# Attention followed by a soft mixture of experts: turned score maxima kept in a score tile's spare columns, a fifth exponential buffer, and PSUM places chosen by two clocks

## The chip, the core and the metric

The kernel runs on one core of one Trainium2 chip. The metric is the device time of one execution in microseconds (us), the median over several runs. Five engines work side by side, each on its own stream of instructions in a fixed order: PE (matrix products and transposes), DVE (vector), ACT (scalar functions), POOL (GpSimd) and SP (issues transfers). They wait for one another through semaphores. PE writes its results to PSUM, and here the kernel divides PSUM into four places of two banks each.

## The reference

```python
scores = scale * np.matmul(q, k.transpose(0, 1, 3, 2))   # 8 batches, 12 heads, 448 rows, depth 64
m = np.max(scores, axis=-1, keepdims=True)
e = np.exp(scores - m)
attn = e / (np.sum(e, axis=-1, keepdims=True) + np.exp(-m) + 1e-09)
x = attn @ v                                             # then x as (3584, 768)
logits = x @ phi                                         # 32 slots
d = softmax of logits over rows;  slot_input = d.T @ x
slot_out = relu(slot_input @ w1[e]) @ w2[e]              # 8 experts, 4 slots each, hidden 1024
out = softmax of logits over slots @ slot_out
```

The two softmaxes of the second half are written out in the reference in the same manner as the first.

## The kernel before

The work of the attention is cut into 24 units. A unit is one pair of batches with one pair of heads, and its 448 rows are cut into 7 blocks of 64. The program runs through *steps*, seven for each unit, and each step issues, in this order, the parts named `small`, the score step, `mid`, `value`, the second score step, `end` and `load` (the loop `for n in range(last + 1)` at the end of the main part). What else belongs to a unit is hung into these parts by the table `SCH`, whose numbers count steps from the unit's first. Each engine's order is this order; nothing reorders it.

The stages that matter here, with the names used below. Position 0 to 6 means the step's place in the cycle of seven.

- **S** (`stage_S`, L340, reduced at L347): PE multiplies a block of query rows with all keys of the unit into one PSUM place, and DVE's `tensor_reduce` takes the row maxima from it. S0 to S6 are the seven of one unit. In the steps that also do value products, S is issued as two *wide* matmuls (64x128 weights), in the others as four of 64x64.
- **T** (`stage_T`, L326, copied by DVE at L327): at position 6, part `value`, PE turns q and k of the *next* unit, and DVE copies them out. S0 of the next unit reads that copy.
- **MT** (`stage_MT`, L354): PE turns the unit's maxima into rows, in four small transposes; ACT copies them out (`mt`, L357), takes `exp(-max)` (`em`, L360), and POOL spreads them out (`md`, L364). ST needs that four steps later. It stands at position 6, part `load`, behind the ST of that step, and takes a PSUM place of its own. The first unit's stands at position 0, part `mid`, by the entry `MT0`.
- **ST** (`stage_ST`, L375 and L380), 11 steps (`LAG`) behind S: PE computes the scores again, turned, with the maxima subtracted, and ACT's exponential at L384 writes them to one of four buffers `et`.
- **AV** (`stage_AV`, L409): PE multiplies the exponentials with the values, 16 small matmuls for each of a unit's seven tiles. `AV0` gives the step of each tile: 15, 15, 16, 17, 18, 19, 19, that is positions 1 (two tiles), 2, 3, 4 and 5 (two tiles), part `mid`, behind S. It holds a PSUM place from the first tile to the copy at L419 (`stage_AVout`).
- **X** (`stage_X`, L487, copied by DVE at L489): at position 6, part `end`, PE turns the finished unit's result.
- **The mixture**: behind every sixth unit, logits, slot softmax and slot inputs are hung into the same steps (L521 to L633). The experts and the output follow when all units are done.

PSUM places are handed out by `slot()`: it takes the place whose `due` is the earliest. In this version `due` is a count of allocations plus a number for each kind. A stage that gets a place waits until the last reader of its former tile is done.

All other working buffers lie in one SBUF tile `block`, at offsets listed in `order`; `rooms` are parts of it that take late weights (`load_late`, L204) as soon as their former content is done with. `pick` is a small constant made once by POOL (L293) and read in the experts' part.

Of the kernel before, what the change touches and what calls it, by code (L numbers as in the profile page):

```python
# [9 lines left out]
F32 = mybir.dt.float32  # L10
BF16 = mybir.dt.bfloat16
# [4 lines left out]

P = 64
LAG = 11
AV0 = (15, 15, 16, 17, 18, 19, 19)
SCH = {'T': (6, 'value'), 'qk': ((2, 'load'), (1, 'mid'), (6, 'end'), (6, 'value')), 'MT': (6, 'load'), 'V': (13, 'mid'), 'v': ((14, 'load'), (17, 'end')), 'AVout': (19, 'mid'), 'N': ((23, 'value'), (23, 'small')), 'X': (27, 'end'), 'mix': (28, ''), 'den': (19, 'load'), 'lp': (29, 'value'), 'last': (21, 'load'), 'Xlast': (24, 'value'), 'k1': (20, 'mid'), 'k2': (30, 'value'), 'k3': (32, 'small'), 'k4': (34, 'load'), 'Xprev': (25, 'value'), 'T0': (1, 'mid'), 'T1': (4, 'value'), 'Vlast': (12, 'end'), 'MT0': (7, 'mid')}  # L20
MIX = {'logits': (0, 'end'), 'slot_max': (5, 'load'), 'slot_exp': (5, 'load'), 'gate_logits': (6, 'value'), 'gate_max': (6, 'value'), 'slots_T': (7, 'mid'), 'gate_exp': (7, 'value'), 'slot_sum': (13, 'small'), 'slot_in': (8, 'load'), 'gate_T': (13, 'end')}
FIN = {'merge_prev': (0, 'load'), 'logits': (1, 'load'), 'slot_max': (2, 'mid'), 'slot_exp': (2, 'value'), 'merge_max': (2, 'value'), 'slots_T': (3, 'mid'), 'merge_acc': (4, 'small'), 'slot_in': (4, 'end'), 'experts_before': (5, 'end'), 'experts_in': (8, 'load'), 'experts_hidden': (10, 'end')}
OPT = {'T': 'dve', 'X': 'dve', 'mt': 'act', 'AVout': 'act', 'pieces': 1, 'S': 'wide', 'raw': 3, 'et': 4, 'lp': 2, 'xt': 3, 'si': 8, 'sin': 3, 'v6': 1, 'late': 1, 'x': 1, 'AV2': 'dve'}
# [7 lines left out]
def kernel(  # L31
# [10 lines left out]
    nc = tc.nc  # L42

    B, H, S, D = q.shape
# [5 lines left out]
    TB = S // P  # L50
# [4 lines left out]
    U = BP * HP  # L55
    C3 = TB // 2
    N2 = 2 * S
# [6 lines left out]
    const = ctx.enter_context(tc.tile_pool(name="const", bufs=1))  # L64
    small = ctx.enter_context(tc.tile_pool(name="small", bufs=2))
# [4 lines left out]
    HW = (KC // 2) * F  # L70
    end, final = TB * U, (U - 1) * TB + SCH["mix"][0]
    lives, count = {}, {}
# [29 lines left out]
    order = [("raw", i) for i in range(3)] + [("x", i) for i in (0, 4, 5, 6)] + [("qk", 0)]  # L102
    order += [("xt", i) for i in range(3)] + [("qk", 1), ("md", 0), ("vr", 0), ("xu", 0), ("qk", 2), ("md", 1)]
    order += [("et", i) for i in range(4)] + [("v6", 0)] + [("x", i) for i in (1, 2, 3)]
    assert sorted(order) == sorted(lives)
    for key in order:
        offs[key] = size
        size += max(-(-lives[key][0] // 16) * 16, N2)


    lives["select", 0], offs["select", 0], count["select"] = (2 * P, U * TB + LAG), offs["md", 1] + 8 * P, 1
# [3 lines left out]
    x22 = R3 + HW  # L115
    R4 = x22 + 4 * N2
    rooms = [0, HW, 2 * HW, R3, R4, R4 + HW, R4 + 2 * HW, x22]
    size = max(size, R4 + 3 * HW)
# [38 lines left out]

    def release():
        due[where["hold"]] = made[0] + LAGS["held"]


    RAW, V65 = {}, {}
# [23 lines left out]
    pieces = 4  # L186
# [91 lines left out]
    def late_constants():  # L278
        shift_masks()
        gdma(out=phi, in_=moe_phi.rearrange("(j p) s -> p j s", p=128))  # L280
        for i in range(4):

            nc.scalar.copy(fold[ds(32 * i, 32), :], ident[ds(32 * i, 32), ds(32 * i, 32)])
        for g in range(G):
            nc.scalar.copy(
                spread[:, g].rearrange("p i (h e k) -> p i h e k", h=G, e=4)[:, :, g],
                ident.rearrange("p (e r k) -> p e r k", e=4, k=SPE)[:, :, 0].unsqueeze(1).broadcast_to([128, 4, 4, SPE]))
        nc.gpsimd.memset(cT[ds(96, 32), :, ds(128, 128)], 0.0)
        nc.vector.tensor_reduce(chunk, ident.rearrange("p (c n) -> p c n", c=4), axis=AX.X, op=ALU.max)
        nc.vector.tensor_reduce(sides, fold.rearrange("p (g n) -> p g n", g=G), axis=AX.X, op=ALU.add)  # L290
        both = [fold[:, ds(16 * g, 16)].rearrange("p (e k) -> p e k", e=4).unsqueeze(2).broadcast_to([128, 4, 8, SPE])
                for g in range(G)]
# [9 lines left out]
    def stage_T(u, bs_=range(2)):  # L302
# [17 lines left out]
        for i, name in enumerate(("qr", "kr")):  # L320
# [6 lines left out]
        (nc.vector.tensor_copy if OPT["T"] == "dve" else nc.scalar.copy)(  # L327
            t_, ps[:, :, ds(0, N2)].rearrange("p i (b n) -> p i b n", b=2))

    def stage_S(u, s):  # L330
        ps = slot([128, 2, 512], kind="S")
        wide = OPT["S"] == "wide" and s < 2 * C3 and u * TB + s in av_steps
        for h in range(2):
            hs = ds(h * D, D)
            for r in range(1 if wide else 2):

                b, o = divmod(s, C3) if s < 2 * C3 else (r, C3)
                o = (o * 128 + r * P + b * P if s < 2 * C3 else o * 128 * (1 - b))
                rs = ds(0, 128) if wide else ds(r * P, P)
                nc.tensor.matmul(ps[rs, h, ds(0, S)], QT[u][hs, b, ds(o, 128 if wide else P)],  # L340
                                 KT[u][hs, b, :], start=True, stop=True)
# [5 lines left out]
        nc.vector.tensor_reduce(m, ps[:, :, ds(0, S)], axis=AX.X, op=ALU.max)  # L347

    def stage_MT(u):
        ps = slot([128, 2, 1024], BF16, "M")  # L350
        for h in range(2):
            for r in range(2):
                rs = ds(r * P, P)
                nc.tensor.transpose(ps[ds(h * D, D), 1 - r, ds(0, P)], M[u % 2][rs, :], ident[rs, rs])  # L354
# [13 lines left out]
        MD[u] = [md[:, ds((1 - b) * P, S)] for b in range(2)]  # L368
# [392 lines left out]
    def at(n, where, f):  # L761
        plan.setdefault((n, where), []).append(f)
# [45 lines left out]
    def run(n, where):  # L808
        for f in plan.pop((n, where), ()):
            f()  # L810

    for n in range(last + 1):
        run(n, "small")
        if n < TB * U:
            stage_S(*divmod(n, TB))
        run(n, "mid")
        run(n, "value")
        if 0 <= n - LAG < TB * U:
            stage_ST(*divmod(n - LAG, TB))
        run(n, "end")  # L820
        run(n, "load")
# [21 lines left out]
    held = []  # L843
# [107 lines left out]
```

## Time and profile before

| | |
|---|---|
| timed runs | 310.0, 311.64 and 312.31 us, median 311.64 |
| span of the profiled execution | 310.7 us; no other time of that execution is given |
| PE, DVE, ACT, POOL busy | 268.8, 250.9, 210.9, 198.3 us |
| 23.65 to 232.38 us, from the second unit's T copy to the last's | 208.73 us for 21 units |
| a unit, T copy to T copy | 9.23 to 11.10 us |

A line of the timeline gives start, duration, engine, line of the kernel, operation, tile written and tile read, and how many instructions were merged; a bracket gives idle time of that engine before it and what ended it. A line of the windows view gives, for a stretch of time, its length and each engine's busy time and instructions, then the granted TensorE clock. A line of the waits view gives who waited for whom: total us, times, longest. Matmuls overlap in PE, so their durations do not add up; the distance between starts is what PE needs.

### The profile page before, as it was taken

To read this page: it belongs to the slowest core of one execution; us is meant where nothing else is said; L and a number is where in the kernel's file an instruction comes from. 1 tells how busy PE (TensorE), PEld (TensorE's weight loads), DVE (VectorE), ACT (ScalarE), POOL (GpSimd) and SP (SyncE) were. 2 spreads that over 40 slices of the span, in tenths; PEclk is the share of its full clock that TensorE was granted. 3 is DMA by queue.
4 is the path that set the end of the run, shared out by engine and by line. 5 is a ranking of instruction groups with operands and counts; after the bars stand their busy time and mean duration, and the time that the engine had idled before them with its cause. 6 is when DMAs were issued, how large, how long until landed. Compare 5 with 4: busy or idle time off the path is not lost.

```text
span 310.7 us, 13686 instructions
## 1 busy us (share of the span) xinstructions
PE 268.8 (87%) x6074; PEld 152.3 (49%) x6074; DVE 250.9 (81%) x323; ACT 210.9 (68%) x309; POOL 198.3 (64%) x342
## 2 busy tenths in 40 slices
PE   2689998999989999999999999999999768996660
PEld 2235555655555555655555555655565444452110
DVE  2998999999989899999999999999999325437560
ACT  1126778777867888877687878887878755426351
POOL 8965787797876787798767977798656551200000
PEclk9999999999999999999999999999999999998555
DMA  6999899989999889989998989999899998947997
GB/s 86 176 158 210 162 180 175 201 174 168 175 178 176 157 128 208 194 175 182 177 168 155 166 159 195 159 213 191 163 162 197 204 170 155 212 84 277 427 420 294
DMA packets 29258, 59.12 MB, mean 190 GB/s; under 512 B 4272, under 2 KB 23216, under 8 KB 29200
## 3 DMA queue, kind: packets, MB, share of 16 engines
q0 software_dynamic: 19728, 36.69, 71.8%
q1 hardware_dynamic: 9472, 21.57, 20.0%
q8 instruction: 47, 0.77, 1.0%
q14 instruction: 11, 0.09, 0.1%
HBM read 83.46 MB, written 11.01 MB: 304 GB/s over the span
## 4 chain that ended last, share of the span: by engine, by line
PE 62%; ACT 12%; DVE 10%; issue 6%; POOL 4%; DMA 4%; ACTq 0%; POOLq 0%; DVEq 0%; SPq 0%
PE ps L409 14%; PE ps L340 11%; PE ps L375 11%; ACT block L384 9%; PE ps L380 8%; PE ps L326 6%; DVE m_sb L347 4%; PE ps L687 4%; DMA out_dram<-wres 3%; PE ps L487 2%; POOL block L167 2%; PE ps L886 2%; DVE wres L895 1%; ACT wres L893 1%; DVE block L327 1%
## 5 line engine op out<-in xcount | busy, mean ns | idle before, releaser
L347 DVE TENSOR_REDUCE m_sb<-ps 128x2 bf16<-128x896 f32 x168 | 179.2, 1088 | 11.1 <-PE ps L340 4.5
L384 ACT ACTIVATE block<-ps 128x896 bf16<-128x896 f32 x168 | 153.7, 918 | 49.9 <-PE ps L380 42.1
L409 PE MATMUL ps<-block 64*128 64x65 bf16 (+1 forms) x2688 | 76.1, 192 | 3.7 <-issue 3.4
L409 PEld LDWEIGHTS <-block 64*128 64x128 bf16 (+1 forms) x2688 | 66.7, 97 | 23.2 <-issue 6.2
L375 PE MATMUL ps<-block 64*64 64x448 bf16 x672 | 69.8, 369 | 2.6 <-DVE acc L499 0.9
L340 PE MATMUL ps<-block 64*64 64x448 bf16 (+1 forms) x452 | 65.4, 386 | 6.2 <-DVE block L317 1.9
L380 PE MATMUL ps<-block 64*64 64x448 bf16 x672 | 66.7, 353 | 0.2 <-issue 0.2
L340 PEld LDWEIGHTS <-block 64*64 64x64 bf16 (+1 forms) x452 | 22.9, 103 | 51.4 <-issue 40.1
L432 POOL TENSOR_TENSOR block<-block,rec 128x384 bf16<-128x384 f32 x46 | 37.3, 835 | 9.0 <-DVE rec L444 7.4
L375 PEld LDWEIGHTS <-block 64*64 64x64 bf16 x672 | 26.4, 106 | 11.9 <-issue 8.6
L167 POOL DMA_DIRECT2D block<-in_k_dram x48 | 30.4, 636 | 1.9 <-PE ps L326 1.9
L167 POOL DMA_DIRECT2D block<-in_q_dram x48 | 30.7, 641 | 0.8 <-POOLq L935 0.8
L195 POOL DMA_DIRECT2D wres<-in_moe_w_dram x48 | 26.5, 553 | 1.7 <-issue 1.7
L364 POOL TENSOR_TENSOR block<-mt,base 128x512 bf16<-128x512 bf16 x23 | 24.3, 1055 | 4.4 <-ACT mt L357 4.0
L326 PEld LDWEIGHTS <-block 128*64 128x64 bf16 x644 | 21.6, 115 | 9.2 <-issue 8.7
L327 DVE COPY block<-ps 128x1792 bf16<-128x1792 bf16 x23 | 24.9, 1082 | 1.4 <-PE ps L326 1.4
L326 PE MATMUL ps<-ident,block 128*64 128x128 bf16 x644 | 24.4, 228 | 1.4 <-issue 1.2
L389 POOL CAST block<-block 128x896 bf16<-128x896 f32 x24 | 22.4, 933 | 4.7 <-DMA block<-in_v_dram 3.3
L425 POOL TENSOR_TENSOR den<-block,em 128x14 f32<-128x14 f32 x23 | 4.9, 212 | 31.7 <-ACT block L419 31.5
L380 PEld LDWEIGHTS <-block 64*64 64x64 bf16 x672 | 24.2, 107 | 0.5 <-issue 0.2
L419 ACT COPY block<-ps 128x910 f32<-128x910 f32 x22 | 20.2, 919 | 1.7 <-PE ps L380 0.4
L895 DVE TENSOR_SCALAR wres<-ps,acc 128x768 f32<-128x768 f32 (+1 forms) x16 | 14.7, 940 | 7.8 <-PE ps L886 5.5
(143 smaller groups left out, 218.8 us busy)
## 6 DMA issues: line engine op xcount, KB each, us to landing
wres<-in_moe_w_dram POOLq DMA_DIRECT2D x48, 384.0 KB, 5.9
block<-in_v_dram SPq DMA_DIRECT2D x46, 224.0 KB, 5.2
out_dram<-wres SPq DMA_DIRECT2D x11, 768.0 KB, 5.4
block<-in_moe_w_dram POOLq DMA_DIRECT2D x8, 768.0 KB, 9.1
block<-in_q_dram POOLq DMA_DIRECT2D x48, 112.0 KB, 4.4
block<-in_k_dram POOLq DMA_DIRECT2D x48, 112.0 KB, 4.6
out_dram<-wres SPq DMA_DIRECT2D x5, 384.0 KB, 5.1
block<-in_v_dram POOLq DMA_DIRECT2D x2, 224.0 KB, 4.4
```

The costliest lines, as they stand in the source:

```text
L167: eng.dma_start(out=t_[ds(b * P, P), :, :], in_=src[bp * 2 + b, ds(hp * 2, 2)].rearrange("h (p t) d -> p h (t d)", t=TB))
L195: gdma(out=t_[rows, ts(half, HW)], in_=src[rows, ts(half, HW)])
L326: nc.tensor.transpose(o[ds(h * D, D)], r[:, h, ts(t, D)], ident)
L327: (nc.vector.tensor_copy if OPT["T"] == "dve" else nc.scalar.copy)(t_, ps[:, :, ds(0, N2)].rearrange("p i (b n) -> p i b n", b=2))
L340: nc.tensor.matmul(ps[rs, h, ds(0, S)], QT[u][hs, b, ds(o, 128 if wide else P)], KT[u][hs, b, :], start=True, stop=True)
L347: nc.vector.tensor_reduce(m, ps[:, :, ds(0, S)], axis=AX.X, op=ALU.max)
L364: (nc.vector if end_ else nc.gpsimd).tensor_tensor(md.rearrange("p (a r n) -> p a r n", a=4, r=2), mt.rearrange("p (r n) -> p r n", r=2).u ...
L375: nc.tensor.matmul(ps[ds(b * P, P), h, ds(0, S)], select[hs, b, :], MD[u][b][hs, :], start=True, stop=False)
L380: nc.tensor.matmul(ps[ds(b * P, P), h, ds(0, S)], KT[u][hs, b, part_of(b, t)], QT[u][hs, b, :], start=False, stop=True)
L384: nc.scalar.activation(et, ps[:, :, ds(0, S)], AF.Exp, scale=scale)
L409: nc.tensor.matmul(o, et[bs, h, ds(c * 128 + b * P if c < C3 else c * 128 * (1 - b), w)], V65[u][bs, h, t, ds(0, 65)], start=(t == 0 and h ...
L432: eng.tensor_tensor(xo[:, ds(b * C3, C3)].rearrange("p c h d -> p h c d"), av[:, b, ds(0, 2 * C3 * 65)].rearrange("p (h c e) -> p h c e", ...
```

## The change

Four edits go together.

1. **The value products start a step later** (`AV0`): 16, 16, 16, 17, 18, 19, 19. Position 1 has no tile any more, position 2 has three. S1 is therefore no longer wide. `et` has five buffers.
2. **MT** moves from position 6, part `load`, to position 0, part `mid`, that is behind S0 of the next unit, and takes no place of its own. It writes into the spare 64 float columns of each bank of that S0 tile. ACT copies from there. The last unit's MT is as before. The first unit's already stood at position 0.
3. **PSUM places** are chosen by two running clocks, one for DVE and one for ACT: each stage adds its time (`LEAVES`) to the clock of the engine that empties it, at 1.36 us a step. Behind the last step the old count is used.
4. **The layout of `block`** is packed anew; `pick` now lies in it and is made later, at step 155.

```diff
-AV0 = (15, 15, 16, 17, 18, 19, 19)
-SCH = {..., 'MT': (6, 'load'), ...}
+AV0 = (16, 16, 16, 17, 18, 19, 19)
+SCH = {..., 'MT': (7, 'mid'), ...}
-OPT = {..., 'et': 4, ...}
+OPT = {..., 'et': 5, ...}
+STEP = 1.36
+LEAVES = {'S': ('DVE', 1.0, 0.8), 'ST': ('ACT', 1.4, 1.04), 'T': ('DVE', 1.1, 1.1), 'X': ('DVE', 3.2, 0.6), 'M': ('ACT', 3.0, 1.1), None: ('ACT', -1.4, 0.1), 'held': ('ACT', 1.4, 1.54)}
...
-    LAGS = {"S": 3, "ST": 3.5, "T": 3, "X": 2.5, "M": 3, "held": 3.5}
-    due, made, where = [0.0] * 4, [0], {}
+    due, made, where, step = [0.0] * 4, [0], {}, [0]
+    clock = {"DVE": 0.0, "ACT": 0.0}
+
+    def leaves(kind):
+        eng, wait, takes = LEAVES[kind if kind in LEAVES else None]
+        clock[eng] = max(clock[eng], step[0] * STEP + wait) + takes
+        return clock[eng]
 
     def slot(shape, dtype=F32, kind=None):
-        made[0] += 1
         i = min(range(4), key=lambda j: (due[j], j))
-        due[i] = made[0] + LAGS.get(kind, 2) if kind != "hold" else float("inf")
         where[kind] = i
+        if step[0] < U * TB + LAG:
+            due[i] = leaves(kind) if kind != "hold" else float("inf")
+            made[0] = step[0] * STEP
+        else:
+            made[0] += 1
+            due[i] = made[0] + 2 if kind != "hold" else float("inf")
         return psum.tile(shape, dtype, tag=f"r{i}", name="ps")
...
+    first_S = {}
+
     def stage_S(u, s):
         ps = slot([128, 2, 512], kind="S")
+        if s == 0:
+            first_S[u] = ps
...
     def stage_MT(u):
-        ps = slot([128, 2, 1024], BF16, "M")
+        ps = (first_S[u + 1].bitcast(BF16)[:, :, ds(2 * S, P)] if u < U - 1 else
+              slot([128, 2, 1024], BF16, "M")[:, :, ds(0, P)])
         for h in range(2):
             for r in range(2):
                 rs = ds(r * P, P)
-                nc.tensor.transpose(ps[ds(h * D, D), 1 - r, ds(0, P)], M[u % 2][rs, :], ident[rs, rs])
+                nc.tensor.transpose(ps[ds(h * D, D), 1 - r, :], M[u % 2][rs, :], ident[rs, rs])
...
-            mt.rearrange("p (r n) -> p r n", r=2), ps[:, :, ds(0, P)])
+            mt.rearrange("p (r n) -> p r n", r=2), ps)
...
-    pick = const.tile([128, 128], F32, name="pick")
+    pick = block[:, ds(pick_at, 256)].bitcast(F32)
...
+    at(free(pick_at, 256), "load", picked)
...
     for n in range(last + 1):
+        step[0] = n
         run(n, "small")
```

`picked()` holds the one POOL instruction that made `pick` before.

More of the change, by code (lines that the diff above doesn't have):

```diff
@@ L18 @@
 LAG = 11
-AV0 = (15, 15, 16, 17, 18, 19, 19)
-SCH = {'T': (6, 'value'), 'qk': ((2, 'load'), (1, 'mid'), (6, 'end'), (6, 'value')), 'MT': (6, 'load'), 'V': (13, 'mid'), 'v': ((14, 'load'), (17, 'end')), 'AVout': (19, 'mid'), 'N': ((23, 'value'), (23, 'small')), 'X': (27, 'end'), 'mix': (28, ''), 'den': (19, 'load'), 'lp': (29, 'value'), 'last': (21, 'load'), 'Xlast': (24, 'value'), 'k1': (20, 'mid'), 'k2': (30, 'value'), 'k3': (32, 'small'), 'k4': (34, 'load'), 'Xprev': (25, 'value'), 'T0': (1, 'mid'), 'T1': (4, 'value'), 'Vlast': (12, 'end'), 'MT0': (7, 'mid')}
+AV0 = (16, 16, 16, 17, 18, 19, 19)
+SCH = {'T': (6, 'value'), 'qk': ((2, 'load'), (1, 'mid'), (6, 'end'), (6, 'value')), 'MT': (7, 'mid'), 'V': (13, 'mid'), 'v': ((14, 'load'), (17, 'end')), 'AVout': (19, 'mid'), 'N': ((23, 'value'), (23, 'small')), 'X': (27, 'end'), 'mix': (28, ''), 'den': (19, 'load'), 'lp': (29, 'value'), 'last': (21, 'load'), 'Xlast': (24, 'value'), 'k1': (20, 'mid'), 'k2': (30, 'value'), 'k3': (32, 'small'), 'k4': (34, 'load'), 'Xprev': (25, 'value'), 'T0': (1, 'mid'), 'T1': (4, 'value'), 'Vlast': (12, 'end'), 'MT0': (7, 'mid')}
 MIX = {'logits': (0, 'end'), 'slot_max': (5, 'load'), 'slot_exp': (5, 'load'), 'gate_logits': (6, 'value'), 'gate_max': (6, 'value'), 'slots_T': (7, 'mid'), 'gate_exp': (7, 'value'), 'slot_sum': (13, 'small'), 'slot_in': (8, 'load'), 'gate_T': (13, 'end')}
 FIN = {'merge_prev': (0, 'load'), 'logits': (1, 'load'), 'slot_max': (2, 'mid'), 'slot_exp': (2, 'value'), 'merge_max': (2, 'value'), 'slots_T': (3, 'mid'), 'merge_acc': (4, 'small'), 'slot_in': (4, 'end'), 'experts_before': (5, 'end'), 'experts_in': (8, 'load'), 'experts_hidden': (10, 'end')}
-OPT = {'T': 'dve', 'X': 'dve', 'mt': 'act', 'AVout': 'act', 'pieces': 1, 'S': 'wide', 'raw': 3, 'et': 4, 'lp': 2, 'xt': 3, 'si': 8, 'sin': 3, 'v6': 1, 'late': 1, 'x': 1, 'AV2': 'dve'}
+OPT = {'T': 'dve', 'X': 'dve', 'mt': 'act', 'AVout': 'act', 'pieces': 1, 'S': 'wide', 'raw': 3, 'et': 5, 'lp': 2, 'xt': 3, 'si': 8, 'sin': 3, 'v6': 1, 'late': 1, 'x': 1, 'AV2': 'dve'}
+STEP = 1.36
+LEAVES = {'S': ('DVE', 1.0, 0.8), 'ST': ('ACT', 1.4, 1.04), 'T': ('DVE', 1.1, 1.1), 'X': ('DVE', 3.2, 0.6), 'M': ('ACT', 3.0, 1.1), None: ('ACT', -1.4, 0.1), 'held': ('ACT', 1.4, 1.54)}
 WRES = 24
@@ L101 @@
     offs, size = {}, 0
-    order = [("raw", i) for i in range(3)] + [("x", i) for i in (0, 4, 5, 6)] + [("qk", 0)]
-    order += [("xt", i) for i in range(3)] + [("qk", 1), ("md", 0), ("vr", 0), ("xu", 0), ("qk", 2), ("md", 1)]
-    order += [("et", i) for i in range(4)] + [("v6", 0)] + [("x", i) for i in (1, 2, 3)]
+    order = [(name[:-1], int(name[-1])) for name in (
+        "raw0 qk0 raw2 raw1 qk1 x1 x2 x3 xt0 xt1 md0 xu0 et3"
+        " vr0 xt2 et4 et0 qk2 md1 v60 et2 et1 x4 x6 x0 x5").split()]
     assert sorted(order) == sorted(lives)
@@ L107 @@
         offs[key] = size
-        size += max(-(-lives[key][0] // 16) * 16, N2)
+        size += -(-lives[key][0] // 16) * 16 + 2 * P * (key == ("md", 1))
     lives["select", 0], offs["select", 0], count["select"] = (2 * P, U * TB + LAG), offs["md", 1] + 8 * P, 1
@@ L117 @@
     rooms = [0, HW, 2 * HW, R3, R4, R4 + HW, R4 + 2 * HW, x22]
-    size = max(size, R4 + 3 * HW)
+    pick_at = R4 + 3 * HW
+    size = max(size, pick_at + 256)
     si_at = x21
@@ L146 @@
     rooms.sort(key=lambda r: free(r, HW))
-    LAGS = {"S": 3, "ST": 3.5, "T": 3, "X": 2.5, "M": 3, "held": 3.5}
-    due, made, where = [0.0] * 4, [0], {}
+    due, made, where, step = [0.0] * 4, [0], {}, [0]
[4 more added lines that the diff above has]
+        return clock[eng]
     def slot(shape, dtype=F32, kind=None):
-        made[0] += 1
         i = min(range(4), key=lambda j: (due[j], j))
-        due[i] = made[0] + LAGS.get(kind, 2) if kind != "hold" else float("inf")
         where[kind] = i
+        if step[0] < U * TB + LAG:
[4 more added lines that the diff above has]
+            due[i] = made[0] + 2 if kind != "hold" else float("inf")
         return psum.tile(shape, dtype, tag=f"r{i}", name="ps")
     def release():
-        due[where["hold"]] = made[0] + LAGS["held"]
+        due[where["hold"]] = leaves("held") if step[0] < U * TB + LAG else made[0] + 3.5
     RAW, V65 = {}, {}
```

1 line of the change is left out of this document (added).

## The prediction

> **What bounds the kernel now.** I read first the page's busy shares, then the windows view to see where the time lies, then the timeline of one unit engine by engine, and last the waits.
>
> ```profile
> PE 268.8 (87%) x6074; PEld 152.3 (49%) x6074; DVE 250.9 (81%) x323; ACT 210.9 (68%) x309; POOL 198.3 (64%) x342
> ...
> L347 DVE TENSOR_REDUCE m_sb<-ps 128x2 bf16<-128x896 f32 x168 | 179.2, 1088 | 11.1 <-PE ps L340 4.5
> L384 ACT ACTIVATE block<-ps 128x896 bf16<-128x896 f32 x168 | 153.7, 918 | 49.9 <-PE ps L380 42.1
> ```
>
> No engine is full over the whole span; the shares mix stages. The stage of the units, 23.65 to 232.38 us, and one tight unit in it are another matter:
>
> ```profile
> 23.65:232.38 208.73, 199.24 (x4935) 117.79 (x4939) 195.53 (x224) 165.51 (x235) 162.98 (x271) 1.00 0.96 176
> 131.17:140.41 9.24, 9.07 (x225) 5.36 (x226) 9.03 (x10) 7.52 (x11) 7.85 (x13) 1.00 0.88 170
> ```
>
> In the tight unit PE is busy 9.07 and DVE 9.03 of 9.24 us: two engines without slack. The clock is 1.00. Whatever makes either wait lengthens the unit. PE's starts in it (S6 of one unit at 130.74, S6 of the next at 139.98, 9.24 us):
>
> ```profile
> 130.74 0.42 PE L340 MATMUL ps<-block 64*64 64x448 bf16 x4
> 131.17 0.97 PE L326 MATMUL ps<-ident,block 128*64 128x128 bf16 x28
> 132.08 0.38 PE L375 MATMUL ps<-block 64*64 64x448 bf16 x4
> ...
> 132.58 0.56 PE L487 MATMUL ps<-ident,block 128*128 128x128 bf16 x7
> 133.08 0.22 PE L354 MATMUL ps<-ident,m_sb 64*64 64x64 bf16 x4
> 133.37 0.38 PE L340 MATMUL ps<-block 64*64 64x448 bf16 x4
> 133.73 0.38 PE L375 MATMUL ps<-block 64*64 64x448 bf16 x4
> ...
> 134.23 0.36 PE L340 MATMUL ps<-block 64*128 64x448 bf16 x2
> 134.43 0.77 PE L409 MATMUL ps<-block 64*128 64x65 bf16 x32
> ...
> 135.52 0.36 PE L340 MATMUL ps<-block 64*128 64x448 bf16 x2
> ...
> 136.67 0.36 PE L340 MATMUL ps<-block 64*128 64x448 bf16 x2
> ```
>
> They are S6, T, ST, X, MT, S0, ST, S1, AV (two tiles), S2, S3. DVE beside it, the T copy, the X copy, then the reductions of S0 and S1 with nothing between:
>
> ```profile
> 132.23 1.08 DVE L327 COPY block<-ps 128x1792 bf16<-128x1792 bf16 x1
> 133.23 0.61 DVE L489 COPY block<-ps 128x896 bf16<-128x896 bf16 x1
> 133.87 2.09 DVE L347 TENSOR_REDUCE m_sb<-ps 128x2 bf16<-128x896 f32 x2
> ```
>
> S1 starts at 134.23, while DVE still reduces S0: that head start of PE keeps DVE full.
>
> **The change part by part.**
>
> *MT.* In the built order of the changed kernel PE has S0, MT, ST, S1, and for the first 23 units MT's first matmul waits for DVE's reduction of that same S0 tile. The wait comes with the place: MT writes into banks that DVE is reading. Before, it waited for an older reduction and had a place of its own. No row of before shows PE writing a bank that is being reduced. The Trainium skill, "PSUM — Partial Sum Buffer", section "PSUM bank collisions raise a hardware error", has the rule that speaks against the edit: guard PSUM by bank and quadrant, not by address, so spare columns of a busy bank are not free. By it the unit grows as worked out next; by addresses alone MT would wait for nothing new and the unit would stay at 9.24.
>
> Worked out from S6 = 0: S0 starts at 2.63 as before (T copy ends 133.31, S0 at 133.37, 0.06 later). DVE's X copy stands ahead, so the reduction of S0 starts at 133.87, that is 3.13, and ends 1.09 later at 4.22. MT starts 0.06 after, at 4.28. What is behind it on PE: ST, S1, ST, S2, the value products. MT itself delays ST little: the first unit's MT in the trace shows both things, PE's wait for a reduction and the next matmul 0.08 us behind.
>
> ```profile
> 14.26 9.07 DVE L347 TENSOR_REDUCE m_sb<-ps 128x2 bf16<-128x896 f32 x9
> ...
> 16.40 0.27 PE L354 MATMUL ps<-ident,m_sb 64*64 64x64 bf16 x4 [2.09 <-DVE m_sb L347]
> 16.48 1.88 PE L340 MATMUL ps<-block 64*64 64x448 bf16 x16
> ```
>
> There DVE went on, since a further S tile stood ready. In the changed order none does. ST starts at 4.36, where it started at 133.73 - 130.74 = 2.99: PE is 1.37 us late. S1 follows 0.50 later (133.73 to 134.23), at 4.86, and its reduction can start about 0.41 after that (at 106.54 a score matmul started, its reduction at 106.95), at 5.27. Before, it started one reduction after 3.13, at about 4.18. DVE stands idle 1.09 us. ACT's exponential waits for the late ST, has 1.7 us of slack in the unit (7.52 of 9.24), and loses nothing of its own. ACT's `mt` and POOL's `md` start 1.9 us later (4.28 against 133.08 - 130.74 = 2.34) for an ST four steps on, which covers it.
>
> *Value products a step later.* S1 to S2 loses two tiles: S to ST 0.36 (133.37 to 133.73) and ST to S 0.50 make 0.86 where it was 1.29. S2 to S3 gains two: its 1.15 plus two tiles of 0.22 to 0.30 (two tiles took 0.59 at 134.43, one 0.30 at 135.72), about 1.60. Net +0.02. The narrow S1 (0.42 against 0.36) is in that. No transfer moves with it.
>
> *Fifth `et` buffer, MT's saved place, the clocks.* What they can give back is DVE's and PE's waiting for places. All idle time of DVE with a named releaser in that stage is 9.8 us, its largest entry
>
> ```profile
> DVE m_sb L347 <- PE ps L340: 3.8, 9, 1.0
> ```
>
> in 9 of 147 reductions. The exponentials never wait for a buffer (ACT's releaser is PE's ST), so the fifth one is worth nothing by itself. Bounds for the three together: a gain of 9.8 us, and a loss where two places come out worse, bounded by one exponential wait: S2 may have to wait for the exponential of the late ST: 4.36 + 0.68 (132.08 to 132.76) + 0.92 + 0.05 = 6.01 instead of 5.72, so 0.29 us a unit. I take a small gain, since the named waits are few.
>
> *Layout and `pick`.* One POOL instruction of 0.39 us leaves the start, where POOL was ahead, for step 155; three of the eight late weight loads start 2 to 4 steps later, but the last ones (step 193) do not move. They are hidden by the experts' start; without that cover, 4 steps of 1.36. Zero.
>
> *Sum.* A tight unit goes from 9.24 to 9.24 + 1.37 + 0.02 = 10.63. The units from 23.65 to 232.38 average 208.73 / 21 = 9.94. Of the 0.70 above 9.24, the mixture's DVE work is about 2.6 us per six units (0.43 each), so 0.27 is waiting, of which I let the new wait swallow half, 0.13. So 22 units at 1.39 - 0.13 = 1.26 make 27.7; the first unit's MT waits one reduction longer without STs in the way, about 0.55. Together 28.2 on the profiled span of 310.7: 338.9. The median of the timed runs is 0.9 above that span; no other time of that execution is shown, so I add it: about 340, and taking 1 us of gain from the places, 339. Low end: DVE's loss alone (1.09) less all the waiting (0.27): 22 x 0.82 = 18, that is 330, and 4 for better places: 326. High end: 1.39 + 0.29 = 1.68 on 22 units, 37, that is 348.
>
> **The rivals.**
>
> *The places pay back.* PE recovers after the stall: steps at 1.15 and 1.12 shrink to the 1.04 that one of them shows (0.30 a unit, 6.6 us), and all 9.8 us of DVE's waits vanish: 339 - 16.4, about 323 (315 to 326). For it: four places, one user fewer. Against it: a step cannot go much below ST to exponential to the next-but-one S (0.68 + 0.92 + 0.05 + 0.20 + 0.30 for two steps, so 1.08 each), and the named waits are scattered. The Trainium skill, "Perfetto Trace Analysis", section "Identifying the Most-Contended Engine", holds that the same bubble repeating on the full engine can mean too little PSUM. This trace shows no repeating one.
>
> *Faster.* MT's wait is free, if PE comes to MT only after the reduction ended. PE would have to arrive at 4.22 instead of about 2.9, 1.3 us late; from there on the wait costs nothing and only the gain remains: 311.6 - 9.8, about 302. Against it: PE waits at S0 for the T copy, so its arrival is tied to DVE, and X copy and reduction always lie between.
>
> *A second gap.* Three tiles of AV between S2 and S3 (1.60) outlast a reduction (1.09). If DVE empties there too and the exponential's wait adds up, 0.5 us a unit more: about 350 (348 to 356). For it: DVE has no stock after the first gap. Against it: PE's own chain already counts these 1.60.
>
> **How the numbers follow.** Forecast 0.80: 339, range 326 to 348. Places pay back 0.08 (323). Second gap 0.05 (350). Faster 0.05 (302). The remaining 0.02: the wait somehow costs only what the places give, within 1%. One per cent is about what a measurement of this kernel can tell from no change. Slower by over 1%: 0.80 + 0.08 + 0.05 = 0.93; same 0.02; faster 0.05. What lies outside the range is 0.20.
>
> **What would show it.** In the changed profile: PE's MT line idle for about 1.2 to 1.5 us with DVE's reduction as releaser, some 23 times; DVE's reduction with PE's S as releaser in each unit, about 1.1 us, together 20 to 25 us; units of about 10.6 us from T copy to T copy; the part behind the units as long as before. Wrong would be: MT without idle time; DVE busy 97% in the units; or units that stay below 10 us.

## The result, and the profile after

The changed kernel takes 340.71 us (median of 4 runs, 338.5 to 342.15); the kernel before, run beside it, 311.65 us (310.0 to 312.31). The ratio is 1.093 (95% interval 1.087 to 1.099): 29 us slower. Executions over 1.5% longer than the fastest of their kernel are left out of the ratios and their intervals, while medians are taken over all. The profiled execution took 338.5 us, the lowest of the four, with a span of 336.7 us, against 310.7 before. Cut at the first and the last T copy of the stage, 26.0 us of span difference lie like this:

| | before | after | difference |
|---|---|---|---|
| ahead of the second unit's T copy | 23.65 | 24.47 | 0.8 |
| 21 units | 208.73 (9.94 each) | 232.64 (11.08 each) | 23.9 |
| behind the last T copy | 78.3 | 79.6 | 1.3 |

First the busy shares of the changed kernel, with its two busiest groups of instructions and the one that the change moved (the columns behind the bars: busy time and mean ns of one, then idle time ahead of them and its releaser):

```profile
PE 265.6 (79%) x6118; PEld 151.8 (45%) x6118; DVE 251.7 (75%) x323; ACT 208.9 (62%) x309; POOL 198.6 (59%) x342
...
L364 DVE TENSOR_REDUCE m_sb<-ps 128x2 bf16<-128x896 f32 x168 | 180.6, 1087 | 34.6 <-PE ps L357 30.5
L402 ACT ACTIVATE block<-ps 128x896 bf16<-128x896 f32 x168 | 152.1, 918 | 43.6 <-PE ps L398 39.5
...
L372 PE MATMUL ps<-ident,m_sb 64*64 64x64 bf16 x96 | 5.4, 208 | 31.9 <-DVE m_sb L364 31.8
```

The work is the same: 168 reductions of 1087 ns, 168 exponentials of 918 ns. What is new is idle time. DVE's reductions now wait 30.5 us for PE's scores (4.5 before), and PE's MT waits 31.8 us for DVE's reductions. The windows view of the stage and of one tight unit shows it as a share (length, then busy time and instructions of PE, PEld, DVE, ACT and POOL, the granted clock, the DMA share and GB/s):

```profile
24.47:257.11 232.64, 195.72 (x4977) 117.45 (x4981) 196.18 (x223) 163.87 (x235) 163.75 (x272) 0.99 0.91 160
145.60:156.21 10.61, 8.84 (x231) 5.33 (x227) 9.14 (x12) 7.48 (x11) 7.88 (x14) 1.00 0.89 157
```

Both engines do the old work (about 196 us of DVE in the stage) in 24 us more. The clock is 0.99 to 1.00, so no throttle is in it. One tight unit, PE first. It begins with S6 at 144.15, and the next S6 is at 154.76, 10.61 us later:

```profile
144.15 0.38 PE L357 MATMUL ps<-block 64*64 64x448 bf16 x4
144.55 0.97 PE L339 MATMUL ps<-ident,block 128*64 128x128 bf16 x28
...
146.74 0.38 PE L357 MATMUL ps<-block 64*64 64x448 bf16 x4 [0.22 <-DVE block L340]
...
148.39 0.22 PE L372 MATMUL ps<-ident,m_sb 64*64 64x64 bf16 x4 [1.27 <-DVE m_sb L364]
148.42 0.39 PE L393 MATMUL ps<-block 64*64 64x448 bf16 x4
...
148.80 0.38 PE L357 MATMUL ps<-block 64*64 64x448 bf16 x4
...
149.49 0.36 PE L357 MATMUL ps<-block 64*128 64x448 bf16 x2
...
150.07 0.96 PE L427 MATMUL ps<-block 64*128 64x65 bf16 x44 [0.22 <-POOL block L382]
...
151.41 0.36 PE L357 MATMUL ps<-block 64*128 64x448 bf16 x2
```

These are S6, T, S0, MT, ST, S1, S2, AV and S3. DVE in the same unit:

```profile
145.60 1.08 DVE L340 COPY block<-ps 128x1792 bf16<-128x1792 bf16 x1
146.60 0.61 DVE L507 COPY block<-ps 128x896 bf16<-128x896 bf16 x1
147.24 1.09 DVE L364 TENSOR_REDUCE m_sb<-ps 128x2 bf16<-128x896 f32 x1
149.23 1.09 DVE L364 TENSOR_REDUCE m_sb<-ps 128x2 bf16<-128x896 f32 x1 [0.90 <-PE ps L357]
...
150.39 1.03 DVE L364 TENSOR_REDUCE m_sb<-ps 128x2 bf16<-128x896 f32 x1
151.81 4.48 DVE L364 TENSOR_REDUCE m_sb<-ps 128x2 bf16<-128x896 f32 x4 [0.40 <-PE ps L357]
```

Read the two together. The reduction of S0 runs from 147.24 to 148.33. PE's MT, issued behind S0, starts at 148.39, 0.06 us after its end, having waited 1.27 us. Only then come ST and, at 148.80, S1. DVE finished S0 at 148.33 and had no further score tile, so it stands idle for 0.90 us until S1, which starts at 148.80 and takes 0.38 us, is there. A second gap of 0.40 us lies ahead of S3's reduction. 0.90 + 0.40 = 1.30 us of DVE in a unit that is 10.61 - 9.24 = 1.37 us longer.

### The profile page after: what moved, and what is told of

It is laid out like the page before. It is cut to its first block, busy times and chain, and to the rows that moved or that the text cites. A ratio compares the mean times of both kernels' runs of the same rounds, so it can differ in the third digit from the quotient of the medians.

```text
span 336.7 us, 13793 instructions
## 1 busy us (share of the span) xinstructions
PE 265.6 (79%) x6118; PEld 151.8 (45%) x6118; DVE 251.7 (75%) x323; ACT 208.9 (62%) x309; POOL 198.6 (59%) x342
## 4 chain that ended last, share of the span: by engine, by line
PE 33%; DVE 22%; POOL 14%; ACT 11%; DMA 10%; issue 8%; POOLq 0%; ACTq 0%; DVEq 0%; SPq 0%
DVE m_sb L364 13%; PE ps L427 11%; ACT block L402 8%; PE ps L357 6%; PE ps L393 6%; POOL block L179 6%; PE ps L398 5%; DMA out_dram<-wres 5%; DMA block<-in_moe_w_dram 5%; DVE block L340 4%; POOL block L382 3%; POOL block L407 2%; ACT block L437 2%; DVE block L507 2%; DVE wres L915 1%
## 5 line engine op out<-in xcount | busy, mean ns | idle before, releaser
L364 DVE TENSOR_REDUCE m_sb<-ps 128x2 bf16<-128x896 f32 x168 | 180.6, 1087 | 34.6 <-PE ps L357 30.5
L402 ACT ACTIVATE block<-ps 128x896 bf16<-128x896 f32 x168 | 152.1, 918 | 43.6 <-PE ps L398 39.5
L393 PE MATMUL ps<-block 64*64 64x448 bf16 x672 | 70.8, 370 | 1.7 <-DVE m_sb L364 0.8
L427 PE MATMUL ps<-block 64*128 64x65 bf16 (+1 forms) x2688 | 69.3, 193 | 2.8 <-POOL block L382 2.2
L427 PEld LDWEIGHTS <-block 64*128 64x128 bf16 (+1 forms) x2688 | 60.7, 98 | 20.8 <-ACT block L402 5.3
L398 PE MATMUL ps<-block 64*64 64x448 bf16 x672 | 67.9, 358 | 1.2 <-issue 1.2
L382 POOL TENSOR_TENSOR block<-mt,base 128x512 bf16<-128x512 bf16 x23 | 23.9, 1038 | 30.3 <-ACT mt L375 27.8
L372 PE MATMUL ps<-ident,m_sb 64*64 64x64 bf16 x96 | 5.4, 208 | 31.9 <-DVE m_sb L364 31.8
L375 ACT COPY mt<-ps 128x128 bf16<-128x128 bf16 x23 | 6.1, 266 | 36.8 <-PE ps L372 36.8
```

The source lines that it names most:

```text
L382: (nc.vector if end_ else nc.gpsimd).tensor_tensor(md.rearrange("p (a r n) -> p a r n", a=4, r=2), mt.rearrange("p (r n) -> p r n", r=2).u ...
L393: nc.tensor.matmul(ps[ds(b * P, P), h, ds(0, S)], select[hs, b, :], MD[u][b][hs, :], start=True, stop=False)
L398: nc.tensor.matmul(ps[ds(b * P, P), h, ds(0, S)], KT[u][hs, b, part_of(b, t)], QT[u][hs, b, :], start=False, stop=True)
L402: nc.scalar.activation(et, ps[:, :, ds(0, S)], AF.Exp, scale=scale)
L427: nc.tensor.matmul(o, et[bs, h, ds(c * 128 + b * P if c < C3 else c * 128 * (1 - b), w)], V65[u][bs, h, t, ds(0, 65)], start=(t == 0 and h ...
```

## The experiments

All times are medians; each ratio is against the kernel before on the same chip, with its 95% interval. "After" and "before" are the two kernels; an edit is given against the one that is named. The kernel before had 310.19, 311.38 and 312.22 us in the three groups of runs.

### MT undone, and MT alone

`e1_mt_own`, after with MT back in its own place and at its old position:

```diff
-        ps = (first_S[u + 1].bitcast(BF16)[:, :, ds(2 * S, P)] if u < U - 1 else
-              slot([128, 2, 1024], BF16, "M")[:, :, ds(0, P)])
+        ps = slot([128, 2, 1024], BF16, "M")[:, :, ds(0, P)]
-SCH = {..., 'MT': (7, 'mid'), ...}
+SCH = {..., 'MT': (6, 'load'), ...}
```

> The changed kernel with MT alone undone: own PSUM place, position 6, part load; value products, five buffers, clocks and layout stay. Theory (the wait of MT for the reduction of the tile it shares is the whole loss): 308 to 314 us, units of 9.2 to 9.8 us from T copy to T copy outside the mixture, no idle time of PE before MT above 3 us in all. Rival (three tiles of value products between S2 and S3, or the clocks, cost part of it): 318 to 335 us, with DVE idle between the reductions of S2 and S3 in each unit.

Measured: 577.45 us, ratio 1.865 (1.851 to 1.879). Both theories missed it, and the run says nothing on MT: it brought in a new fault. In the two clocks M is entered with 1.1 us on ACT's, and that entry had been used once; now it comes in every unit. Seven ST at 1.04, one `held` at 1.54 and one M at 1.1 make 9.92 us of ACT's clock in a unit of 7 x 1.36 = 9.52 us. The modelled clock runs away by 0.4 us a unit, the `due` of ACT's tiles lies ever farther in the future, and PE is sent into places that DVE is still reading. (That this entry is the fault, `e9_mt_own_due` below shows: with it taken away, the same kernel takes 316.4 us.) The waits view:

```profile
PE ps L392 <- DVE m_sb L364: 68.7, 94, 1.3
```

That is a wait of ST for a reduction, 94 times; in after, the ST line's idle time put down to the reductions is 0.8 us in all.

`e2_mt_alone`, before with MT alone moved and put into S0's spare columns (old layout, old `AV0`, old counting):

```diff
...
-        ps = slot([128, 2, 1024], BF16, "M")
+        ps = (first_S[u + 1].bitcast(BF16)[:, :, ds(2 * S, P)] if u < U - 1 else
+              slot([128, 2, 1024], BF16, "M")[:, :, ds(0, P)])
...
-SCH = {..., 'MT': (6, 'load'), ...}
+SCH = {..., 'MT': (7, 'mid'), ...}
```

> The kernel before with MT alone changed: position 0, part mid, spare columns of the next unit's first score tile; all else as before. Theory: 1.2 to 1.4 us in each of 22 units, 336 to 343 us, PE idle before MT 28 to 34 us in all with DVE's reduction as releaser. Rival (the loss needs the moved value products too, because two tiles at position 1 give DVE a second score tile sooner or later): 318 to 332 us.

Measured: 342.64 us, ratio 1.104 (1.094 to 1.114). That lies in the theory's 336 to 343 us. This one edit alone costs as much as the whole change, and its waits are those of after, on the corresponding lines:

```profile
PE ps L359 <- DVE m_sb L351: 32.0, 23, 3.0
DVE m_sb L351 <- PE ps L344: 26.8, 31, 1.3
```

`e3_move_alone`, before with only the position changed; MT keeps a place of its own:

```diff
-SCH = {..., 'MT': (6, 'load'), ...}
+SCH = {..., 'MT': (7, 'mid'), ...}
```

> The kernel before with MT at position 0, part mid, but in a PSUM place of its own. It tells the move from the sharing. Theory: 309 to 316 us, since MT waits only for the unit's last reduction, which is done, and for its place. Rival (standing behind S0, and so ahead of one more ST, is what costs): 325 us or more.

Measured: 325.0 us, ratio 1.048 (1.040 to 1.057). The theory missed it; the time is just what the rival asked for, but not for the rival's reason. PE's timeline in a unit of this kernel, DVE's, and a line of the waits view:

```profile
136.90 0.20 PE L354 MATMUL ps<-ident,m_sb 64*64 64x64 bf16 x4
...
138.34 0.72 PE L409 MATMUL ps<-block 64*128 64x65 bf16 x28 [0.42 <-DVE m_sb L347]
```

```profile
137.19 2.09 DVE L347 TENSOR_REDUCE m_sb<-ps 128x2 bf16<-128x896 f32 x2
...
139.84 5.64 DVE L347 TENSOR_REDUCE m_sb<-ps 128x2 bf16<-128x896 f32 x5 [0.41 <-PE ps L340]
```

```profile
PE ps L409 <- DVE m_sb L347: 6.9, 16, 0.8
```

MT waits for nothing here, and S0 and S1 are reduced without a gap (x2 at 137.19). So MT at this position, behind S0 and ahead of ST, costs nothing as long as it has a place of its own. But the count of allocations has shifted by one. By the built order AV is now given the place of S0 in 16 of the 24 units. In the unit shown it waits 0.42 us for that reduction, and DVE is empty 0.41 us ahead of S2's. The tightest units are 9.83 us long instead of 9.24, and the 21 units average 10.35 instead of 9.94. So the order in which places go round has a price of its own, and e3 does not show the move by itself.

### The same with the fault of e1 taken away

`e9_mt_own_due` is e1 with M's `due` set without advancing ACT's clock; the other three use the same line where M has a place or a tile of its own.

```diff
-            due[i] = leaves(kind) if kind != "hold" else float("inf")
+            due[i] = float("inf") if kind == "hold" else step[0] * STEP + 4.1 if kind == "M" else leaves(kind)
```

> The first experiment once more (changed kernel, MT undone), but MT's own place gets a due of its step's time plus 4.1 us and no longer advances ACT's clock. In the first run the clock gained 7 x 1.04 + 1.54 + 1.1 = 9.92 us a unit against 7 x 1.36 = 9.52 of the steps, 0.4 us more in each unit, and units grew from 10 to 24 us. Theory (MT's wait is the whole loss of the change, the clock's drift that of the first run): 307 to 314 us, no unit above 11.5 us. Rival (three tiles of value products or five buffers cost too): 318 to 335 us, DVE idle between the reductions of S2 and S3.

Measured: 316.4 us, ratio 1.014 (1.009 to 1.019), 2.4 us above the theory's range and 1.6 below the rival's; one unit is 11.52 us long. Everything of the change but MT's new tile and position is in this kernel, so those two together are worth 340.7 - 316.4 = 24.3 us, or 1.10 us on each of 22 units. (MT takes a place of its own in it, so the places go round otherwise than in after; e10 below, with as few allocations as after in all units but one, is no slower for it.) The waits of e9, DVE's side of one unit, and the windows of its 21 units and of that one unit:

```profile
DVE m_sb L364 <- PE ps L357: 8.8, 19, 0.7
PE ps L371 <- DVE m_sb L364: 2.3, 2, 2.1
```

```profile
143.62 0.62 DVE L506 COPY block<-ps 128x896 bf16<-128x896 bf16 x1
144.26 2.09 DVE L364 TENSOR_REDUCE m_sb<-ps 128x2 bf16<-128x896 f32 x2
146.26 0.23 DVE L461 RECIPROCAL rec<-den 128x14 f32<-128x14 f32 x1
146.41 5.59 DVE L364 TENSOR_REDUCE m_sb<-ps 128x2 bf16<-128x896 f32 x5
```

```profile
23.23:232.76 209.53, 195.68 (x4969) 119.02 (x4973) 194.25 (x224) 162.44 (x235) 163.50 (x271) 1.00 0.94 176
142.62:151.91 9.29, 9.02 (x231) 5.53 (x227) 9.04 (x11) 7.36 (x11) 7.87 (x14) 1.00 0.99 190
```

Seven reductions without one gap, in a unit of 9.29 us, although the value products lie a step later here too.

The first try at the next question, `e4_own_tile`, carried the fault of e1: after, with MT at its old position in the spare columns of its *own* unit's S6.

```diff
-        if s == 0:
+        if s == TB - 1 and 0 < u < U - 1:
             first_S[u] = ps
+            own[u] = where["S"]
+            due[own[u]] = float("inf")
...
-        ps = (first_S[u + 1].bitcast(BF16)[:, :, ds(2 * S, P)] if u < U - 1 else
+        ps = (first_S[u].bitcast(BF16)[:, :, ds(2 * S, P)] if u in own else
...
+        if u in own:
+            due[own[u]] = leaves("M")
-SCH = {..., 'MT': (7, 'mid'), ...}
+SCH = {..., 'MT': (6, 'load'), ...}
```

> The changed kernel with MT at position 6, part load, in the spare columns of its own unit's last score tile, which is held until then. It shares a bank with a reduction too, but with the one whose result it needs anyway. Theory (only a reduction that is still ahead costs): 307 to 313 us, PE idle before MT under 3 us. Rival (writing into a tile that DVE has just read costs by itself, or the longer hold of that place does): 318 us or more.

Measured: 532.51 us, ratio 1.720 (1.708 to 1.733), for the reason of e1. `e10_own_tile_due` is the same with `due[own[u]] = step[0] * STEP + 4.1`.

> MT in the spare columns of its own unit's last score tile, position 6, part load, again with a due of 4.1 us that leaves ACT's clock alone. Theory (a shared bank costs nothing when the reduction is one that MT needs anyway): the same as with a place of its own, 307 to 314 us, PE idle before MT under 3 us in all. Rival (sharing a bank costs by itself): 320 us or more.

Measured: 314.38 us, ratio 1.009 (1.004 to 1.013), 0.4 us above the theory's range and far from the rival's 320. Sharing a score tile is thus no cost in itself. S6's maxima belong to the unit that MT turns, so MT has to wait for that very reduction in any case; S0's belong to the next unit, and MT needs nothing of them.

`e11_step_later`: after, with MT one position on, behind S1, still in S0's spare columns (the tile is held until then):

```diff
-SCH = {..., 'MT': (7, 'mid'), ...}
+SCH = {..., 'MT': (8, 'mid'), ...}
...
+                own[u] = where["S"]
+                due[own[u]] = float("inf")
...
+            due[own[u + 1]] = step[0] * STEP + 2.2
...
```

> The changed kernel with MT in the same spare columns (next unit's first score tile), but one step later: position 1, part mid, behind S1; the tile is held until then. PE still waits, about 0.5 us a unit (S1 at 3.49 after S6, reduction's end at 4.22), but DVE has S1 in stock. Theory: units of about 9.75 us, 314 to 322 us, DVE not idle between the reductions of S0 and S1. Rival (the wait costs what it costs, wherever it stands): 335 us or more.

Measured: 323.09 us, ratio 1.035 (1.029 to 1.042), 1.1 us above the theory's range; the rival had 335 or more. MT still waits, but behind S1 instead of ahead of it. PE, then DVE:

```profile
146.96 0.36 PE L360 MATMUL ps<-block 64*64 64x448 bf16 x4
148.01 0.22 PE L375 MATMUL ps<-ident,m_sb 64*64 64x64 bf16 x4 [0.70 <-DVE m_sb L367]
```

```profile
146.87 2.09 DVE L367 TENSOR_REDUCE m_sb<-ps 128x2 bf16<-128x896 f32 x2
...
150.48 3.29 DVE L367 TENSOR_REDUCE m_sb<-ps 128x2 bf16<-128x896 f32 x3 [0.43 <-PE ps L360]
```

S1 (146.96) is out before MT waits, and DVE reduces S0 and S1 in one run of 2.09 us. PE still loses 14.2 us to this wait in all (31.8 in after), yet 17.6 of the 24.3 us are gone. What is left of the cost, 323.1 - 316.4 = 6.7 us, goes with the gap of 0.43 us that now stands ahead of the reductions of S3 and on.

`e12_half`: after, with MT in S0's spare columns in the 11 odd units alone; the even ones keep the old way.

```diff
-        ps = (first_S[u + 1].bitcast(BF16)[:, :, ds(2 * S, P)] if u < U - 1 else
+        ps = (first_S[u + 1].bitcast(BF16)[:, :, ds(2 * S, P)] if u % 2 and u < U - 1 else
...
-        put(u, "MT" if u else "MT0", lambda u=u: stage_MT(u))
+        at(u * TB + (7 if u % 2 or not u else 6), "mid" if u % 2 or not u else "load", lambda u=u: stage_MT(u))
```

> Half the dose: MT shares the next unit's first score tile in the 11 odd units only; the others have it at position 6, part load, in a place of their own with the due of 4.1 us. Theory (a fixed price for each shared tile): half way between the run with MT undone and the changed kernel, 322 to 329 us, odd units about 1.3 us longer than even ones. Rival (the loss comes from the places or the value products, in all units): above 334 us, or units alike.

Measured: 329.12 us, ratio 1.053 (1.047 to 1.059). Midway between e9 and after is (316.4 + 340.7) / 2 = 328.6. The units alternate in the trace, for instance 9.28 and 10.61 us, and MT waits in half of them:

```profile
PE ps L372 <- DVE m_sb L364: 17.2, 12, 2.1
```

The cost sits in each sharing unit by itself; it is not a state that the whole pipeline falls into.

### The rest of the change

`e13_layout_only` is before with the packed layout, five `et` and `pick` in `block` made at step 155. `e14_layout_av` adds the shifted value products to it. `e15_clocks_only` is before with the two clocks in place of the count (M's `due` as in e9). `e16_own_clocks` is e15 with MT in its own S6, without the layout.

```diff
-OPT = {..., 'et': 4, ...}
+OPT = {..., 'et': 5, ...}
...
-    pick = const.tile([128, 128], F32, name="pick")
+    pick = block[:, ds(pick_at, 256)].bitcast(F32)
...
```

> The kernel before with the new layout of the block tile alone: packed offsets, the fifth buffer, the small constant inside. Theory (in the packed layout the late expert weights may start later and closer together, the last of them lands later, and PE waits for it): 313 to 317 us, the units as long as before, PE 2 to 3.5 us idle in the experts' part with a transfer of late weights as releaser. Rival (the layout is free, as predicted, and the run with MT undone was longer for another reason): 309.5 to 312.5 us, no such wait.

Measured: 314.16 us, ratio 1.017 (1.011 to 1.023).

```diff
-AV0 = (15, 15, 16, 17, 18, 19, 19)
+AV0 = (16, 16, 16, 17, 18, 19, 19)
```

> The same with the value products a step later as well, PSUM places still counted the old way. Theory (the moved value products cost next to nothing, 0.02 us a unit): within 2 us of the run with the layout alone, 313 to 319 us. Rival (three tiles between S2 and S3 open a gap in DVE): 0.3 us or more a unit, 320 us or more.

Measured: 315.7 us, ratio 1.017 (1.012 to 1.022).

```diff
...
-        due[i] = made[0] + LAGS.get(kind, 2) if kind != "hold" else float("inf")
...
+            due[i] = float("inf") if kind == "hold" else step[0] * STEP + 4.1 if kind == "M" else leaves(kind)
...
```

> The kernel before with PSUM places by the two clocks alone, MT's due 4.1 us behind its step and outside the clocks. Theory (few waits are for places): 309 to 312 us. Rival (the clocks win back a good part of the 9.8 us of named idle time): below 308 us.

Measured: 311.59 us, ratio 1.001 (0.996 to 1.005).

```diff
...
-        ps = slot([128, 2, 1024], BF16, "M")
+        ps = (first_S[u].bitcast(BF16)[:, :, ds(2 * S, P)] if u in own else
+              slot([128, 2, 1024], BF16, "M")[:, :, ds(0, P)])
...
```

> The version the runs so far point to: the kernel before, its layout and value products, with the clocks and with MT in the spare columns of its own unit's last score tile. Theory (MT took that tile's place in most units anyway, so nothing is saved and nothing lost): 308 to 312 us. Rival (one allocation fewer a unit and the clocks together remove waits): below 307 us, DVE's waits for PE's S under 2 us in all.

Measured: 313.77 us, ratio 1.011 (1.007 to 1.015), 1.8 us above the theory's range. The rival's gain is not there: DVE waits 7.9 us for PE's S in all, where the rival had under 2.

So the clocks bring nothing (e15), the value products' step costs nothing that shows (e14 against e13), and the packed layout, taken together with the fifth buffer and `pick`, seems to cost something by itself. Its mark is in the late weights. The waits of after and of e13 have a line that before does not have:

```profile
PE ps L705 <- DMA block<-in_moe_w_dram: 2.2, 1, 2.2
```

```profile
PE ps L690 <- DMA block<-in_moe_w_dram: 1.9, 1, 1.9
```

The experts' first products wait for a late weight. Counted from the last T copy, before issues the last six of the eight transfers 13.8, 19.4, 25.5, 26.7, 32.0 and 32.6 us behind it; after 19.7, 22.6, 23.5, 24.7, 30.0 and 30.6 us, so six of them within 11 us instead of 19. The view of that line's transfers, of before, of after and of e13:

```profile
DMA to landing us min/median/max: 6.5/9.1/11.5
```

```profile
DMA to landing us min/median/max: 6.7/9.3/15.3
```

```profile
DMA to landing us min/median/max: 7.6/10.4/14.9
```

In the chain of after that ended last, one of them stands as a single piece (start, us, what):

```profile
287.73 15.26 DMA block<-in_moe_w_dram
303.02 1.46 PE ps L705 x29
```

In e15 and e16, with the old layout, the longest landing is 10.6 and 11.4 us, and PE has no such wait. A long landing is not the layout's alone, though: it is 13.2 us in e2 and 12.9 in e3, both with the old layout, but there PE waits 0.2 us and not at all.

How much of this reaches the end, the traces show in part. From the end of the last of the 168 exponentials (L384 of before) to the end of the span it is 52.8 us in before, 53.3 in e2, 53.0 in e3 and 52.8 in e16, all with the old layout, and 55.0 in e13, 56.1 in after, 57.4 in e10 and 58.4 in e9, all with the packed one. In e13, whose units are as long as before's (9.91 us on average against 9.94), the 2.2 us stand beside the 1.9 us that PE waits for a late weight. After, e9 and e10 come to that exponential about 2 us sooner behind the last T copy (23.5, 23.5 and 23.4 us against 25.6), which gives part of it back; no run shows why. In whole times it stays small: e13 is 1.1 to 2.3% slower than before, and e10 with the packed layout stands no farther from before (1.009) than e16 without it (1.011).

No version was faster than before; e15 is level with it.

## Why the prediction was right, step by step

**MT's wait for the bank that is being reduced: right, in place and size.** Set from S6 = 0, as the prediction did:

| | predicted | measured (144.15 = 0) |
|---|---|---|
| S0 starts | 2.63 | 2.59 |
| its reduction starts, ends | 3.13, 4.22 | 3.09, 4.18 |
| MT starts | 4.28 | 4.24 |
| ST starts | 4.36 | 4.27 |
| S1 starts, its reduction | 4.86, 5.27 | 4.65, 5.08 |
| DVE idle ahead of it | 1.09 (5.27 - 4.22 is 1.05) | 0.90 |
| S1 to S2, S2 to S3 | 0.86, 1.60 | 0.69, 1.92 |
| the tight unit | 10.63 | 10.61 |

e2 and e9 hold it from both sides: the edit of MT alone makes a loss as large as the whole change, and without it the tight unit is back at 9.29. Its cost there is 10.61 - 9.29 = 1.32 us, where the prediction had 1.37. That it is the wait, and not the move, e3 and e11 bear out: at the same position with a place of its own MT waits for nothing (e3), and one position on, where S1 is out before MT waits, most of the cost is gone (e11). The Trainium skill, "PSUM — Partial Sum Buffer", section "PSUM bank collisions raise a hardware error", would have a program guard by bank and not by address. The trace agrees with the part of it that bears on time: MT's columns are not those that DVE reads, and PE waits 1.27 us for the reduction all the same. Whether the program guards by the bank or by the whole tile, and what would come without that guard, no run here shows.

**ST to S1, and S2 to S3: two small sizes off, against one another.** ST came 0.03 behind MT, not 0.08, and S1 0.38 behind ST, not 0.50, so DVE idled 0.90. (The prediction's 1.09 is how much later than before S1's reduction starts; by its own times the idle stretch is 5.27 - 4.22 = 1.05.) S2 came 0.69 behind S1, not 0.86. What both had won was given back between S2 and S3 (1.92 against 1.60): AV starts 0.58 behind S2 where it was 0.20 before, after a wait of 0.22. The trace puts that down to POOL's `md`, which AV does not read; the exponential of the late ST, whose place AV takes by the built order, ends beside it at about 150.0. That would be the bound of 0.29 that the prediction laid on S2, met by AV instead; no run here separates the two.

**How much of the old waiting the new wait swallows: mis-sized.** The prediction took half, 0.13 of 0.27. The 0.27 was too small: by the windows that it shows, DVE was busy 195.53 / 21 = 9.31 us in an average unit and 9.03 in the tight one, so of the 0.70 between them the mixture's work is 0.28, not 0.43, and 0.42 is waiting. The tight unit grew by 1.32 from e9 to after, the average one by (232.64 - 209.53) / 21 = 1.10, so 0.22 went. That is about half, as the prediction took it, but half of more. It makes 22 x 1.10 = 24.2 us of the 27.7 that were forecast. The first unit's part was right: MT's longest wait went from 2.1 to 2.8 us, 0.7 against 0.55.

**Value products a step later: right.** 0.02 us a unit was forecast, and e14 does not differ from e13. The fifth buffer is what the later step needs by the built order: with four, the ST of a unit's step 15 would write over the tile that AV reads at step 16. No run shows it by itself.

**Places and clocks: nothing, where 1 us of gain was taken.** e15 is at 1.001. MT's saved place is worth nothing either (e16 1.011, e10 1.009): in 14 of 24 units of before, by the built order, MT had taken the place of S6, whose reduction it waits for in any case.

**Layout at "Zero": wrong in kind.** The prediction said that three of the late weights start later, that the last ones "do not move" and that all "are hidden by the experts' start". The starts came as said (the last pair 30.0 us behind the last T copy, 32.0 before), but the later ones now fall together with the rest, the longest landing grows from 11.5 to 15.3 us, and PE waits 2.2 us for it. A transfer was priced by its start alone.

**The part behind the last T copy: not "as long as before".** It is 1.3 us longer in after (79.6 against 78.3), and the prediction's own count of 22 units asked for that. Only 21 of the 22 units of the sum lie between the two T copies; the 22nd wait of MT stands behind the last one, which starts at 257.11:

```profile
259.90 0.22 PE L372 MATMUL ps<-ident,m_sb 64*64 64x64 bf16 x4 [1.27 <-DVE m_sb L364]
```

The rest of that part nearly cancels: with this wait in it, the stretch up to the last exponential is 2.0 us shorter than before (23.5 against 25.6), and the one behind it 3.3 longer (56.1 against 52.8).

**The total came out closer than its terms, and that is luck.** MT's edit gave 24.3 us for about 28, and all the rest cost 1.4% (0.9 to 1.9, by e9), about 4 us, for a forecast gain of 1 us. In the profiled execution of e9 those 4 us lie behind the last T copy (81.9 us against 78.3); its 21 units take 209.5 us against 208.7. The span alone was forecast at 337.9 and was 336.7; the 0.9 us between span and median became 4.0: 1.8 between the span and the time of the same execution, and 2.2 from that execution, the lowest of the four, to the median.

**The rivals.** "The places pay back" fell with e15. "Faster" asked that PE come to MT 1.3 us late; MT waits 1.27 us in the unit shown. "A second gap" is there in the trace (0.40 us ahead of S3's reduction) but does not add: S3 starts at 7.26 where 5.72 + 1.60 = 7.32 was forecast, so the gap only takes back what S1 and S2 had won. It does add to DVE's waits, which come to 30.5 us in all where 20 to 25 were foretold. The sentence of the Trainium skill on repeating bubbles, which the first rival draws on, stands in "Perfetto Trace Analysis" under "Optimization Strategy". None of the three had what e3 showed, that moving one allocation by one step turns the round of the places and costs 4.8% without any sharing.

## What to carry to other kernels

When an edit makes the engine that feeds another wait for what that other is doing *now*, ask how many finished pieces lie between them: if none, the wait of the one (1.27 us) is followed by a gap of the other (0.90 us), and the unit grows by 1.32 us though not one operation became longer. The same shared tile costs nothing where the waiting operation needs that reduction anyway (e10), and much less one piece later, when the next piece is already out (e11). Try each edit of a bundle by itself, and when places are chosen by modelled clocks, add up the model's rates first: 0.4 us a period too much was enough for 577 us.

## What the runs showed that was not expected

In e1 the units grow from 10.2 to 27 us, and the granted TensorE clock falls with it. The windows view of e1, from 24 to 200 us, and of after, 100 to 200:

```profile
24.00:100.00 76.00, 55.07 (x1267) 32.20 (x1267) 51.37 (x55) 42.62 (x58) 43.11 (x71) 0.93 0.75 141
100.00:200.00 100.00, 69.05 (x1003) 36.88 (x1003) 40.07 (x46) 34.67 (x49) 32.37 (x53) 0.52 0.39 70
```

```profile
100.00:200.00 100.00, 85.35 (x2222) 52.05 (x2211) 86.65 (x102) 73.63 (x110) 72.31 (x121) 1.00 0.92 159
```

PE is busy 69% of the time at a clock of 0.52, with ST's first matmuls at 556 ns instead of 362, and does less than half of the instructions; in after 85% busy keeps 1.00, although MT makes PE stand still for 1.27 us in every unit. The longest wait that the trace names for PE's matmuls in that stretch of e1 is 1.3 us, of its weight loads 1.7. So many short waits go with the lower clock here; which of them, or how much of them together, brings it down was not tried. A wrong order of places can cost twice in this way: the waits themselves, and then every matmul.
